# Decode attention on one core: K in whole 64 KB descriptors with two buffers, one V buffer, V through four column tiles, most of wo as rows

## The chip, the cores and the metric

The kernel runs on one core of a Trainium2 chip. The metric is the device time of one execution in microseconds. The kernel before takes 663.1 us. The experiments ran in four calls on different chips, each with the kernel before beside it (medians 663.20, 663.03, 663.14 and 663.18); the control of the changed kernel belongs to the first call alone. The profile of a run shows one of its executions, often the slowest.

## The reference

Two rows of one token each go through a pre-norm attention block with a cached K and V and then through a gated MLP:

```python
B, Sq, D = 2, 1, 512;  Hq = Hkv = 32;  Sk = 8192;  Dh = 128;  F = 1376       # bf16
q      = (layernorm(x) @ wq)                 # 32 heads of 128
scores = einsum("bhqd,bhkd->bhqk", q, k) * Dh ** -0.5
o      = einsum("bhqk,bhkd->bhqd", softmax(scores), v)
h      = x + o @ wo
n      = layernorm(h)
g      = n @ W_gate;  g = g * (g > 0)
out    = h + (g * (n @ W_up)) @ W_down
```

K and V together are 268 MB of the 281 MB that are read. Each element is used once.

## The kernel before

Four heads make a "quad": 8.4 MB of K and as much of V. 4 x 8192 keys lie over 128 partitions, T = 256 keys in each, so a quad of K or of V takes 64 KB of a partition; HT is half of T. There are N = 16 quads. A descriptor is one contiguous piece of a load, here what one partition gets; the trace shows each as a packet of that size. DVE multiplies K with the query and adds pairwise; ScalarE takes the exponential into `pm`; TensorE multiplies `pm` with V (of the two operands of a matmul, the stationary one is loaded first and the moving one streams past it). All loads are issued in program order by one queue (SP), and each waits there until its buffer is free (SPq in the views is that queue's sequencer).

```python
ring = ctx.enter_context(tc.tile_pool(name="ring", bufs=3))     # K, V, wq and the weights W by turns
...
def load_k(n):
    kts[n] = load(A_k_cache, n, (0, HT, T))                     # two DMAs, 32 KB a partition each
def load_v(n, cuts=(0, T)):
    vts[n] = load(A_v_cache, n, cuts)                           # one DMA, 64 KB a partition

def scores(n, k, lo, hi, between=None):                         # on half a quad
    ...
    nc.vector.tensor_tensor(out=kt[:, lo:hi, :], in0=kt[:, lo:hi, :], in1=<query>, op=ALU.mult)
    width = Dh
    while width > 8:
        half = width // 2
        nc.vector.tensor_tensor(<first half of width> += <second half>)
        width = half
    nc.vector.tensor_reduce(out=sc[:, 0:w], in_=<the last 8>, axis=AXIS.X, op=ALU.add)
    ...                                                         # exponentials into pm on ScalarE

def v_moving(n, o, lo, hi):                                     # V streams, pm is stationary
    for t in range(lo, hi, TG):                                 # TG = 4 keys of 4 heads: 16 columns
        ts = slice(t, t + TG)
        nc.tensor.matmul(out=o, lhsT=pm[:, ts, :].rearrange("p t h -> p (t h)"),
                         rhs=vt[:, ts, :].rearrange("p t d -> p (t d)"),
                         start=(t == 0), stop=(t == T - TG))
...
for n in range(N - 1):
    if n < N - 2:
        load_k(n + 1)
    scores(n, 0, 0, HT, between.get(n))
    scores(n, 1, HT, T)
    if n < N - 3:
        load_v(n + 1)
    ret = weighted_v(n)
    ...                                # at n == N - 3: V(N-2) and K(N-1) by halves, interleaved
...                                    # then wo, the last V in four pieces, W_gate, W_up, W_down
scores(N - 1, 0, 0, HT); scores(N - 1, 1, HT, CUTS[2], ...); scores(N - 1, 2, CUTS[2], T)
for i in range(LQ):
    for j in range(J):
        project(wo_sb[:, i, j, :], oc[:, i, j, :], ...)          # 4 x 28 matmuls of 2 columns
v_stationary(...)                                                # the last V, by pieces
...                                                              # second layernorm, MLP, store
```

The softmax here doesn't subtract the row's maximum and nothing guards it: scores larger than these inputs give would overflow.

## Time and profile before

| | before |
|---|---|
| time, median of 3 | 663.12 us (662.98 to 663.18) |
| span in the profile | 661.4 us |
| DMA busy, share of 16 engines | 99.0% |
| DVE busy | 603.0 us, 91% |
| TensorE busy | 295.7 us, 45% |

The first part of the profile page, as lines: busy time (share of the span) and instructions; then rows of the 40 slices, each digit the busy tenths of one slice (16.5 us); then the DMA packets and the queue that all loads use.

```profile
span 661.4 us, 4235 instructions
PE 295.7 (45%) x1704; PEld 132.7 (20%) x1704; DVE 603.0 (91%) x244; ACT 84.9 (13%) x329; POOL 4.7 (1%) x19
...
DVE  1698999999999999999999999999999999999991
...
DMA  9999999999999999999999999999999999999996
GB/s 381 444 444 411 450 406 442 428 449 444 398 443 426 450 414 453 418 426 442 415 462 409 430 442 421 452 414 447 420 428 444 425 460 400 436 424 436 412 410 256
DMA packets 10715, 281.32 MB, mean 425 GB/s; under 512 B 996, under 2 KB 1608, under 8 KB 4040
...
q1 hardware_dynamic: 10692, 281.06, 99.0%
```

Both rows are full of nines. Which of the two limits? Two views decide. The groups of instructions show in the last column how long an engine was idle just before, and for whom:

```profile
L251 PE MATMUL o<-kv,pm 128*16 128x512 bf16 x960 | 248.1, 424 | 322.4 <-DMA kv<-in_A_v_cache_dram 290.6
L202 DVE TENSOR_TENSOR kv<-kv,qrep 128x16384 bf16<-128x16384 bf16 (+2 forms) x33 | 278.1, 8427 | 29.3 <-DMA kv<-in_A_k_cache_dram 29.0
```

DVE and TensorE both wait for DMA. Does DMA wait for them? The queue's own table of waits (waiter, releaser: us in all, times, longest) seems to say yes:

```profile
SPq L183 <- DVE sc L217: 415.5, 14, 40.7
SPq L183 <- PE o L251: 124.0, 14, 10.4
```

But the sequencer that issues loads waits well before its engines run dry. The records of the single DMA packets, in the trace, settle it (this is a count over these records, not a view of the profile):

```
                              before
first packet starts           1.84 us
busy, mean of the 16 engines  654.8 us
first / last engine done      655.8 / 657.3 us
packets of 32 KB, median      1216 ns (x4608)
packets of 64 KB, median      2422 ns (x1792)
```

1.84 + 654.83 is 656.7, between the ends of the first and the last engine, so the engines had no idle time to speak of before their end. The end itself, in the timeline (start, length, engine, line, instruction; in brackets the idle time before it and what ended it):

```profile
650.82 1.71 PE L430 MATMUL gate_ps<-hd,W 128*128 128x2 bf16 x44 [0.25 <-DVE hd L416]
...
653.31 1.75 PE L430 MATMUL up_ps<-hd,W 128*128 128x2 bf16 x44 [0.35 <-DMA W<-in_B_W_up_dram]
...
656.93 0.99 PE L458 MATMUL y_ps<-act,W 128*128 128x2 bf16 x24 [0.80 <-DMA W<-in_B_W_down_dram]
...
659.39 0.30 SPq L476 DMA_DIRECT2D out_dram<-y_row  x1
```

The matmuls with W_gate (called the gate below) start at 650.82 us. Those with W_up and W_down wait for DMA, and some 4.5 us follow the last of these waits.

### The profile page before, as it was taken

To read this page: it belongs to the slowest core of one execution; us is meant where nothing else is said; L and a number is where in the kernel's file an instruction comes from. 1 tells how busy PE (TensorE), PEld (TensorE's weight loads), DVE (VectorE), ACT (ScalarE), POOL (GpSimd) and SP (SyncE) were. 2 spreads that over 40 slices of the span, in tenths; PEclk is the share of its full clock that TensorE was granted. 3 is DMA by queue.
4 is the path that set the end of the run, shared out by engine and by line. 5 is a ranking of instruction groups with operands and counts; after the bars stand their busy time and mean duration, and the time that the engine had idled before them with its cause. 6 is when DMAs were issued, how large, how long until landed. Compare 5 with 4: busy or idle time off the path is not lost.

```text
span 661.4 us, 4235 instructions
## 1 busy us (share of the span) xinstructions
PE 295.7 (45%) x1704; PEld 132.7 (20%) x1704; DVE 603.0 (91%) x244; ACT 84.9 (13%) x329; POOL 4.7 (1%) x19
## 2 busy tenths in 40 slices
PE   2108245090633608264370915537081552844346
PEld 1003112030211203122140301213030120311246
DVE  1698999999999999999999999999999999999991
ACT  2111101111101111110111110111111101111110
POOL 2000000000000000000000000000000000000000
PEclk9757669586776957777595867859586785956755
DMA  9999999999999999999999999999999999999996
GB/s 381 444 444 411 450 406 442 428 449 444 398 443 426 450 414 453 418 426 442 415 462 409 430 442 421 452 414 447 420 428 444 425 460 400 436 424 436 412 410 256
DMA packets 10715, 281.32 MB, mean 425 GB/s; under 512 B 996, under 2 KB 1608, under 8 KB 4040
## 3 DMA queue, kind: packets, MB, share of 16 engines
q1 hardware_dynamic: 10692, 281.06, 99.0%
q8 instruction: 13, 0.21, 0.1%
q14 instruction: 6, 0.05, 0.0%
q10 hardware_dynamic: 4, 0.00, 0.0%
HBM read 281.05 MB, written 0.00 MB: 425 GB/s over the span
## 4 chain that ended last, share of the span: by engine, by line
DVE 45%; DMA 41%; PE 8%; SPq 3%; ACT 2%; issue 1%; DVEq 0%
DMA kv<-in_A_k_cache_dram 34%; DVE kv L209 21%; DVE kv L202 21%; PE o L251 7%; DMA W<-in_A_wo_dram 3%; DVE sc L217 3%; SPq L370 3%; DMA W<-in_B_W_down_dram 2%; DMA wq_sb<-in_A_wq_dram 2%; ACT pm L234 2%; PE qps L164 1%; DVE ou L285 0%; SPq L376 0%; DVE rep L282 0%; PE y_ps L458 0%
## 5 line engine op out<-in xcount | busy, mean ns | idle before, releaser
L251 PE MATMUL o<-kv,pm 128*16 128x512 bf16 x960 | 248.1, 424 | 322.4 <-DMA kv<-in_A_v_cache_dram 290.6
L202 DVE TENSOR_TENSOR kv<-kv,qrep 128x16384 bf16<-128x16384 bf16 (+2 forms) x33 | 278.1, 8427 | 29.3 <-DMA kv<-in_A_k_cache_dram 29.0
L209 DVE TENSOR_TENSOR kv<-kv 128x8192 bf16<-128x8192 bf16 (+5 forms) x132 | 276.8, 2097 | 4.4
L251 PEld LDWEIGHTS <-pm 128*16 128x16 bf16 x960 | 91.9, 98 | 474.1 <-issue 295.8
L234 ACT ACTIVATE pm<-sc 32x128 bf16<-32x128 f32 (+1 forms) x128 | 61.6, 481 | 427.9 <-DVE sc L217 426.4
L217 DVE TENSOR_REDUCE sc<-kv 128x128 f32<-128x1024 bf16 (+2 forms) x33 | 39.2, 1188 | 3.3
L234 ACT ACTIVATION_READ_ACCUMULATOR pm<-sc 32x1 f32 x128 | 31.8, 248 | 0.0
L261 ACT ACTIVATE osb<-o,turn_of 16x128 f32<-16x128 f32 x60 | 16.6, 347 | 112.2 <-PE o L251 105.0
L275 PE MATMUL rep<-osb,head_of 16*128 16x128 f32 x112 | 17.2, 292 | 7.2 <-ACT osb L261 7.2
L275 PEld LDWEIGHTS rep<-osb,head_of 16*128 16x128 f32 x112 | 14.5, 183 | 14.2 <-ACT osb L261 13.1
L292 PE MATMUL o_b<-pm,kv 128*128 128x4 bf16 x256 | 7.4, 166 | 6.6 <-DMA kv<-in_A_v_cache_dram 6.6
L292 PEld LDWEIGHTS <-kv 128*128 128x128 bf16 x256 | 7.3, 105 | 6.9 <-DMA kv<-in_A_v_cache_dram 6.9
L386 PE MATMUL a_ps<-oc,W 128*128 128x2 bf16 x112 | 3.1, 165 | 11.7 <-DVE oc L313 11.7
L164 PE MATMUL qps<-wq_sb,xnb 128*32 128x512 bf16 x64 | 5.5, 517 | 4.5 <-DMA wq_sb<-in_A_wq_dram 4.5
L386 PEld LDWEIGHTS <-W 128*128 128x128 bf16 x128 | 3.7, 104 | 12.0 <-DMA W<-in_A_wo_dram 7.6
L164 PEld LDWEIGHTS <-xnb 128*32 128x32 bf16 x64 | 2.7, 119 | 6.9 <-issue 5.4
L430 PEld LDWEIGHTS <-W 128*128 128x128 bf16 (+1 forms) x88 | 3.4, 122 | 0.7 <-DMA W<-in_B_W_up_dram 0.4
L170 ACT ACTIVATE qrep<-qps 128x512 bf16<-128x512 f32 x4 | 2.4, 598 | 6.0 <-PE qps L164 6.0
L318 DVE RECIPROCAL zil<-zb 128x4 f32<-128x4 f32 x2 | 0.4, 178 | 2.9 <-PE zb L297 2.9
L137 PE MATMUL x_ps<-ident,x_row 2*128 2x2 bf16 x4 | 0.4, 173 | 5.8 <-DMA x_row<-in_A_x_dram 5.8
L297 PE MATMUL zb<-zl,mean_f 128*128 128x4 f32 x12 | 2.8, 354 | 0.0
L297 PEld LDWEIGHTS zb<-zl,mean_f 128*128 128x128 f32 x12 | 2.8, 329 | 0.0
(82 smaller groups left out, 40.5 us busy)
## 6 DMA issues: line engine op xcount, KB each, us to landing
kv<-in_A_k_cache_dram SPq DMA_DIRECT2D x32, 4096.0 KB, 32.3
kv<-in_A_v_cache_dram SPq DMA_DIRECT2D x3, 4096.0 KB, 21.3
wq_sb<-in_A_wq_dram SPq DMA_DIRECT2D x1, 4096.0 KB, 12.3
W<-in_A_wo_dram SPq DMA_DIRECT2D x1, 3584.0 KB, 21.2
kv<-in_A_v_cache_dram SPq DMA_DIRECT2D x1, 2560.0 KB, 26.0
W<-in_B_W_gate_dram SPq DMA_DIRECT2D x1, 1376.0 KB, 29.3
W<-in_B_W_up_dram SPq DMA_DIRECT2D x1, 1032.0 KB
kv<-in_A_v_cache_dram SPq DMA_DIRECT2D x1, 1024.0 KB, 27.2
```

Source lines behind the costliest of these rows:

```text
L164: nc.tensor.matmul(out=qps[h * Q:(h + 1) * Q], lhsT=xnb[:, c, b, :], rhs=wq_v[:, c, g:g + QP, h, :], start=(c == 0), stop=(c == KC - 1),)
L202: nc.vector.tensor_tensor(out=kt[:, lo:hi, :], in0=kt[:, lo:hi, :], in1=_view(qrep[:, b, i, :], 0, [[0, w], [1, Dh]]), op=ALU.mult)
L209: nc.vector.tensor_tensor(out=_view(kt, off, [[Dh, w], [1, half]]), in0=_view(kt, off, [[Dh, w], [1, half]]), in1=_view(kt, off + half, [[ ...
L217: nc.vector.tensor_reduce(out=sc[:, 0:w], in_=_view(kt, off, [[Dh, w], [1, 8]]), axis=AXIS.X, op=ALU.add)
L234: nc.scalar.activation(out=pm[ps, lo:hi, h], in_=sc[ps, 0:w], func=ACT.Exp, accum_out=(zm[ps, b, k, i:i + 1] if i < LQ else zl[ps, b, k, h ...
L251: nc.tensor.matmul(out=o, lhsT=pm[:, ts, :].rearrange("p t h -> p (t h)"), rhs=vt[:, ts, :].rearrange("p t d -> p (t d)"), start=(t == 0), ...
L261: nc.scalar.activation(out=osb[:, t, :], in_=o[:, t, :], func=ACT.Copy, scale=turn_of[:, t:t + 1])
L275: nc.tensor.matmul(out=reps[i // HQ][:, i % HQ, :], lhsT=head_of.rearrange("k h m -> k (h m)"), rhs=osb[:, t, :], start=(t == 0), stop=(t ...
L292: nc.tensor.matmul(out=o, lhsT=vt[:, t, :], rhs=pm[:, t, :], start=(t == 0), stop=(t == T - 1))
L297: nc.tensor.matmul(out=zb, lhsT=lhsT, rhs=z[:, k, :], start=(k == 0), stop=(k == 2))
L370: nc.sync.dma_start(out=wgu[:, g, c0:c1, :], in_=w.rearrange("(c p) n -> p c n", p=P)[:, c0:c1, :])
L386: nc.tensor.matmul(out=a_ps[:, c, :], lhsT=w[:, c * P:(c + 1) * P], rhs=o, start=(first and c == 0), stop=last, skip_group_check=True)
```

## The change

Its intent: K in whole loads, so in descriptors of 64 KB like V; two K buffers of their own, each refilled as soon as its scores are done, so that K runs a quad ahead of V; one buffer for V, made affordable by putting its matmuls through four column tiles of TensorE by turns (a tile is one of four groups of 32 output partitions, `g` in the code); DVE on whole quads (fewer instructions); and most of `wo` as 28 matmuls with 512 moving columns, also column-tiled, instead of 112 small ones. Core of the diff, cuts marked:

```diff
-    ring = ctx.enter_context(tc.tile_pool(name="ring", bufs=3))
+    kring = ctx.enter_context(tc.tile_pool(name="kring", bufs=2))
+    vring = ctx.enter_context(tc.tile_pool(name="vring", bufs=1))
 ...
-    def load_k(n):
-        kts[n] = load(A_k_cache, n, (0, HT, T))
+    def load_k(n):
+        kts[n] = kring.tile([P, T, Dh], bf16, tag="k", name="k")
+        load_part(kts[n], A_k_cache, n, 0, T)
 ...                                   scores(n, k, lo, hi, ...) becomes scores(n), on all of T
+    def clear(o):
+        nc.tensor.matmul(out=o, lhsT=<zeros>, rhs=<zeros>, start=True, stop=False, ...)
+
     def v_moving(n, o, lo, hi):
-        for t in range(lo, hi, TG):
+        for k, t in enumerate(range(lo, hi, TG)):
             ts = slice(t, t + TG)
-            nc.tensor.matmul(out=o, lhsT=pm[:, ts, :].rearrange("p t h -> p (t h)"),
+            g = k % (P // Q) * Q                       # column tile 0, 1, 2, 3, 0, ...
+            nc.tensor.matmul(out=o[g:g + G * TG], lhsT=pm[:, ts, :].rearrange("p t h -> p (t h)"),
 ...
     load_k(0)
+    load_k(1)
     load_v(0)
     for n in range(N - 1):
-        if n < N - 2:
-            load_k(n + 1)
-        scores(n, 0, 0, HT, between.get(n))
-        scores(n, 1, HT, T)
-        if n < N - 3:
-            load_v(n + 1)
+        scores(n)
+        if n + 2 < N:
+            load_k(n + 2)
         ret = weighted_v(n)
+        if n + 2 < N:
+            load_v(n + 1)
 ...
-    scores(N - 1, 0, 0, HT)
-    scores(N - 1, 1, HT, CUTS[2], most_of_last_row)
-    scores(N - 1, 2, CUTS[2], T)
-    for i in range(LQ):
-        for j in range(J):
-            project(wo_sb[:, i, j, :], oc[:, i, j, :], first=(i == 0 and j == 0))
+    scores(N - 1)
+    gather(HQ, LQ)
+    normalize(L, zb1)
+    ar_ps = ps_mm.tile([P, D], f32, tag="mm")
+    clear(ar_ps)
+    for k in range(LQ * J):                            # wo as rows, four column tiles
+        g = k % (P // Q) * Q
+        nc.tensor.matmul(out=ar_ps[g:g + B], lhsT=oc[:, k // J, k % J, :],
+                         rhs=wo_sb[:, k // J, k % J, :], start=False, ...)
+    ar = ...copy of ar_ps...
+    v_moving(N - 1, o15, 0, CUTS[1])
+    ...eight f32 matmuls bring ar back into a_ps...
+    v_moving(N - 1, o15, CUTS[1], CUTS[2])
 ...                                   the last 48 of 256 keys stay stationary, as before
```

More of the change, by code (lines that the diff above doesn't have):

```diff
@@ L59 @@
     misc = ctx.enter_context(tc.tile_pool(name="misc", bufs=1))
-    ring = ctx.enter_context(tc.tile_pool(name="ring", bufs=3))
-    spool = ctx.enter_context(tc.tile_pool(name="spool", bufs=2))
+    kring = ctx.enter_context(tc.tile_pool(name="kring", bufs=2))
+    vring = ctx.enter_context(tc.tile_pool(name="vring", bufs=1))
+    spool = ctx.enter_context(tc.tile_pool(name="spool", bufs=1))
     opool = ctx.enter_context(tc.tile_pool(name="opool", bufs=1))
@@ L68 @@
     mean_f = consts.tile([P, P], f32)
-    zm = consts.tile([P, B, 3, NQ - 1], f32)
-    zl = consts.tile([P, B, 3, G], f32)
+    zm = consts.tile([P, B, NQ - 1], f32)
+    zl = consts.tile([P, B, G], f32)
     eps_t = consts.tile([P, 1], f32)
@@ L80 @@
     masks.make_identity(nc, ident)
-    head_of = consts.tile([G * TG, G, Q], f32)
-    nc.gpsimd.memset(head_of, 0.0)
-    for t in range(TG):
-        nc.gpsimd.affine_select(out=head_of, in_=head_of, compare_op=ALU.not_equal, fill=1.0,
-                                base=-G * t, pattern=[[-1, G], [0, Q]], channel_multiplier=1)
-    turn_of = consts.tile([G * TG, TG], f32)
-    nc.gpsimd.memset(turn_of, 1.0)
+    head_of = consts.tile([P, G, Q], f32)
+    turn_of = consts.tile([P, TG], f32)
+    row_of = consts.tile([P, B], f32)
+    for t in (head_of, turn_of, row_of):
+        nc.gpsimd.memset(t, 0.0)
+    for g in range(P // Q):
+        for u in range(TG):
+            for t, base, pat in ((head_of, G * u, [[-1, G], [0, Q]]), (turn_of, u, [[-G, TG]])):
+                nc.gpsimd.affine_select(out=t, in_=t, compare_op=ALU.not_equal, fill=1.0,
+                                        base=-(Q * g + base), pattern=pat, channel_multiplier=1)
+        nc.gpsimd.affine_select(out=row_of, in_=row_of, compare_op=ALU.not_equal, fill=1.0,
+                                base=-Q * g, pattern=[[-1, B]], channel_multiplier=1)
+    zero = consts.tile([P, 1], bf16)
+    nc.gpsimd.memset(zero, 0.0)
     same = consts.tile([P, G, Q], f32)
     nc.gpsimd.memset(same, 1.0)
-    for t, pat, n in ((turn_of, [[G, TG]], G), (same, [[Q, G], [0, Q]], Q)):
-        neg = [[-s_, c_] for s_, c_ in pat]
-        nc.gpsimd.affine_select(out=t, in_=t, compare_op=ALU.is_ge, fill=0.0, base=0,
-                                pattern=neg, channel_multiplier=1)
-        nc.gpsimd.affine_select(out=t, in_=t, compare_op=ALU.is_ge, fill=0.0, base=n - 1,
-                                pattern=pat, channel_multiplier=-1)
-    mine = consts.tile([P, G], bf16)
-    nc.vector.tensor_copy(mine, same[:, :, 0])
+    nc.gpsimd.affine_select(out=same, in_=same, compare_op=ALU.is_ge, fill=0.0, base=0,
+                            pattern=[[-Q, G], [0, Q]], channel_multiplier=1)
+    nc.gpsimd.affine_select(out=same, in_=same, compare_op=ALU.is_ge, fill=0.0, base=Q - 1,
+                            pattern=[[Q, G], [0, Q]], channel_multiplier=-1)
     pick = consts.tile([P, Q], f32)
@@ L111 @@
     RING = T * Dh
-    wq_sb = ring.tile([P, RING], bf16, tag="s", name="wq_sb")[:, 0:KC * Hq * Dh].rearrange(
+    wq_sb = vring.tile([P, RING], bf16, tag="v", name="wq_sb")[:, 0:KC * Hq * Dh].rearrange(
         "p (c n) -> p c n", c=KC)
@@ L174 @@
     N = len(seq)
-    HT = T // 2
     LQ = NQ - 1
@@ L183, in load_part, with load_v, scores @@
         nc.sync.dma_start(out=t[:, lo:hi, :], in_=src[:, lo:hi, :])
-    def load(cache, n, cuts):
-        t = ring.tile([P, T, Dh], bf16, tag="s", name="kv")
-        for lo, hi in zip(cuts[:-1], cuts[1:]):
-            load_part(t, cache, n, lo, hi)
-        return t
-    def load_k(n):
-        kts[n] = load(A_k_cache, n, (0, HT, T))
-    def load_v(n, cuts=(0, T)):
-        vts[n] = load(A_v_cache, n, cuts)
-    def scores(n, k, lo, hi, between=None):
-        b, i = seq[n]
-        kt, w = kts[n], hi - lo
-        off = lo * Dh
-        nc.vector.tensor_tensor(out=kt[:, lo:hi, :], in0=kt[:, lo:hi, :],
-                                in1=_view(qrep[:, b, i, :], 0, [[0, w], [1, Dh]]), op=ALU.mult)
-        if between is not None:
-            between()
+    def load_k(n):
+        kts[n] = kring.tile([P, T, Dh], bf16, tag="k", name="k")
+        load_part(kts[n], A_k_cache, n, 0, T)
+    def load_v(n, cuts=(0, T)):
+        vts[n] = vring.tile([P, T, Dh], bf16, tag="v", name="v")
+        for lo, hi in zip(cuts[:-1], cuts[1:]):
+            load_part(vts[n], A_v_cache, n, lo, hi)
+    def scores(n):
+        b, i = seq[n]
+        kt = kts[n]
+        nc.vector.tensor_tensor(out=kt, in0=kt, in1=_view(qrep[:, b, i, :], 0, [[0, T], [1, Dh]]),
+                                op=ALU.mult)
         width = Dh
@@ L208, in scores @@
             half = width // 2
-            nc.vector.tensor_tensor(
-                out=_view(kt, off, [[Dh, w], [1, half]]),
-                in0=_view(kt, off, [[Dh, w], [1, half]]),
-                in1=_view(kt, off + half, [[Dh, w], [1, half]]),
-                op=ALU.add,
-            )
+            nc.vector.tensor_tensor(out=kt[:, :, 0:half], in0=kt[:, :, 0:half],
+                                    in1=kt[:, :, half:width], op=ALU.add)
             width = half
-        sc = spool.tile([P, HT], f32, name="sc")
-        nc.vector.tensor_reduce(out=sc[:, 0:w], in_=_view(kt, off, [[Dh, w], [1, 8]]),
-                                axis=AXIS.X, op=ALU.add)
+        sc = spool.tile([P, T], f32, name="sc")
+        nc.vector.tensor_reduce(out=sc, in_=kt[:, :, 0:8], axis=AXIS.X, op=ALU.add)
         pm = pms[n % NM]
-        if n == N - 1 and hi == T:
-            pd = misc.tile([P, w], bf16)
-            zd = misc.tile([P, 1], f32)
-            nc.scalar.activation(out=pd, in_=sc[:, 0:w], func=ACT.Exp, accum_out=zd,
-                                 scale=SCALE)
-            nc.vector.tensor_tensor(out=pm[:, lo:hi, :],
-                                    in0=pd.unsqueeze(2).to_broadcast([P, w, G]),
-                                    in1=_view(mine, 0, [[0, w], [1, G]]), op=ALU.mult)
-            nc.vector.tensor_tensor(out=zl[:, b, k, :], in0=same[:, :, 0],
-                                    in1=zd.to_broadcast([P, G]), op=ALU.mult)
-            return
         for h in range(G):
             ps = slice(h * Q, (h + 1) * Q)
-            nc.scalar.activation(out=pm[ps, lo:hi, h], in_=sc[ps, 0:w], func=ACT.Exp,
-                                 accum_out=(zm[ps, b, k, i:i + 1] if i < LQ
-                                            else zl[ps, b, k, h:h + 1]), scale=SCALE)
+            nc.scalar.activation(out=pm[ps, :, h], in_=sc[ps, :], func=ACT.Exp,
+                                 accum_out=(zm[ps, b, i:i + 1] if i < LQ else zl[ps, b, h:h + 1]),
+                                 scale=SCALE)
     oc = misc.tile([P, LQ, J, B], bf16)
@@ L244, with blocks_of @@
     reps = {}
+    def clear(o):
+        nc.tensor.matmul(out=o, lhsT=_view(zero, 0, [[0, P]]), rhs=_view(zero, 0, [[0, TG * Dh]]),
+                         start=True, stop=False, skip_group_check=True)
     def v_moving(n, o, lo, hi):
         vt, pm = vts[n], pms[n % NM]
-        for t in range(lo, hi, TG):
+        for k, t in enumerate(range(lo, hi, TG)):
             ts = slice(t, t + TG)
-            nc.tensor.matmul(out=o, lhsT=pm[:, ts, :].rearrange("p t h -> p (t h)"),
+            g = k % (P // Q) * Q
+            nc.tensor.matmul(out=o[g:g + G * TG], lhsT=pm[:, ts, :].rearrange("p t h -> p (t h)"),
                              rhs=vt[:, ts, :].rearrange("p t d -> p (t d)"),
-                             start=(t == 0), stop=(t == T - TG))
+                             start=False, stop=(t + P // Q * TG >= hi), skip_group_check=True)
+    def blocks_of(o):
+        osb = opool.tile([P, TG, Dh], f32, tag="row", name="osb")
+        for t in range(TG):
+            nc.scalar.activation(out=osb[:, t, :], in_=o[:, t * Dh:(t + 1) * Dh], func=ACT.Copy,
+                                 scale=turn_of[:, t:t + 1])
+        return osb
     def weighted_v(n):
         b, i = seq[n]
-        o = ps_o.tile([G * TG, TG, Dh], f32, tag="o", name="o")
+        o = ps_o.tile([P, TG * Dh], f32, tag="o", name="o")
+        clear(o)
         v_moving(n, o, 0, T)
-        osb = opool.tile([G * TG, TG, Dh], f32, tag="row", name="osb")
-        for t in range(TG):
-            nc.scalar.activation(out=osb[:, t, :], in_=o[:, t, :], func=ACT.Copy,
-                                 scale=turn_of[:, t:t + 1])
+        osb = blocks_of(o)
         if i == LQ:
@@ L292, in v_stationary @@
             nc.tensor.matmul(out=o, lhsT=vt[:, t, :], rhs=pm[:, t, :],
-                             start=(t == 0), stop=(t == T - 1))
+                             start=(t == CUTS[2]), stop=(t == T - 1), skip_group_check=True)
     def sum_z(zb, lhsT, z):
-        for k in range(3):
-            nc.tensor.matmul(out=zb, lhsT=lhsT, rhs=z[:, k, :], start=(k == 0), stop=(k == 2))
+        nc.tensor.matmul(out=zb, lhsT=lhsT, rhs=z, start=True, stop=True)
         return zb
@@ L334 @@
     load_k(0)
+    load_k(1)
     load_v(0)
     for n in range(N - 1):
-        if n < N - 2:
-            load_k(n + 1)
-        scores(n, 0, 0, HT, between.get(n))
-        scores(n, 1, HT, T)
-        if n < N - 3:
-            load_v(n + 1)
-        ret = weighted_v(n)
-        if n == N - 3:
-            vts[n + 1], kts[n + 2] = (ring.tile([P, T, Dh], bf16, tag="s", name="kv")
-                                      for _ in range(2))
-            for lo, hi in ((0, HT), (HT, T)):
-                load_part(vts[n + 1], A_v_cache, n + 1, lo, hi)
-                load_part(kts[n + 2], A_k_cache, n + 2, lo, hi)
+        if n in between:
+            between[n]()
+        scores(n)
+        if n + 2 < N:
+            load_k(n + 2)
+        ret = weighted_v(n)
+        if n + 2 < N:
+            load_v(n + 1)
         if n == NQ - 1:
@@ L353 @@
             zb0, zl0 = row_z(0, z0[:, 0:LQ]), last_z(0, z0[:, LQ:])
-    W = ring.tile([P, RING], bf16, tag="s", name="W")
+    W = kring.tile([P, RING], bf16, tag="k", name="W")
     wo_sb = W[:, 0:LQ * J * D].rearrange("p (i j n) -> p i j n", j=J, n=D)
@@ L366 @@
     nc.sync.dma_start(out=wol, in_=A_wo[LQ * G * Dh:, :].rearrange("(h d) n -> d h n", d=P))
-    CUTS = (0, HT, T * 13 // 16, T * 15 // 16, T)
+    CUTS = (0, T // 2, T * 13 // 16, T * 15 // 16, T)
     load_v(N - 1, CUTS)
@@ L382, with project @@
     a_ps = ps_acc.tile([P, KC, B], f32)
-    def project(w, o, first=False, last=False):
+    def project(w, o, last):
         for c in range(KC):
             nc.tensor.matmul(out=a_ps[:, c, :], lhsT=w[:, c * P:(c + 1) * P], rhs=o,
-                             start=(first and c == 0), stop=last, skip_group_check=True)
+                             start=False, stop=last, skip_group_check=True)
     L = B - 1
     zb1 = row_z(L, z_tile()[:, 0:LQ])
-    def most_of_last_row():
-        gather(HQ, LQ)
-        normalize(L, zb1)
-    scores(N - 1, 0, 0, HT)
-    scores(N - 1, 1, HT, CUTS[2], most_of_last_row)
-    scores(N - 1, 2, CUTS[2], T)
-    for i in range(LQ):
-        for j in range(J):
-            project(wo_sb[:, i, j, :], oc[:, i, j, :], first=(i == 0 and j == 0))
+    scores(N - 1)
[6 more added lines that the diff above has]
+        nc.tensor.matmul(out=ar_ps[g:g + B], lhsT=oc[:, k // J, k % J, :],
+                         rhs=wo_sb[:, k // J, k % J, :], start=False,
+                         stop=(k + P // Q >= LQ * J), skip_group_check=True)
+    ar = opool.tile([P, D], f32, tag="row")
+    nc.scalar.activation(out=ar, in_=ar_ps, func=ACT.Copy)
+    o15 = ps_o.tile([P, TG * Dh], f32, tag="o")
+    clear(o15)
+    v_moving(N - 1, o15, 0, CUTS[1])
+    for c in range(KC):
+        nc.tensor.matmul(out=a_ps[:, c, :], lhsT=ar[:, c * P:(c + 1) * P], rhs=row_of,
+                         start=(c == 0), stop=False, skip_group_check=True)
+    v_moving(N - 1, o15, CUTS[1], CUTS[2])
+    osb = blocks_of(o15)
     o_b = ps_o.tile([P, G], f32, tag="o", name="o_b")
-    v_stationary(N - 1, o_b, 0, CUTS[2])
     v_stationary(N - 1, o_b, CUTS[2], CUTS[3])
     zil = invert_last(L, last_z(L, z_tile()[:, 0:G]))
+    for t in range(TG):
+        nc.tensor.matmul(out=o_b, lhsT=osb[:, t, :], rhs=head_of[:, :, 0], start=False, stop=False,
+                         skip_group_check=True)
     v_stationary(N - 1, o_b, CUTS[3], T)
```

## The prediction

> **What bounds the kernel now.** The DMA queue. The page's slices show DMA at 9 tenths or more in 39 of 40, the queue table 99.0% of the span. By the trace's packet records the first packet starts at 1.84 us, each engine is busy 654.83 us, and the last W_down lands at about 656.9: 1.84 + 654.83 = 656.7, so there are no bubbles to speak of. Then 4.5 us of down projection, transpose and store follow (timeline). DVE is 91% busy, but its 29 us of waits on K (table of waits) are starvation: a quad costs DVE 37.5 us (chain of waits, 63.0 to 100.5), and DMA about 38.8 for its K and V.
>
> **What the change does.**
> - K in 64 KB descriptors. Packet medians: 1216 ns for 32 KB, 2422 for 64 KB (V has these already). Two of 32 KB cost 10 ns more than one of 64; 2176 pairs over 16 engines: 1.4 us, with fewer semaphore packets and hiccups some 0.2 more. The Trainium skill, "DMA: Bandwidth & Descriptors", Specifications, gives a fabric ceiling of 435 GB/s; the trace's 64 KB packets make 433, so little is left to win.
> - DVE in whole quads. Sizes 16384, 10240 and 6144 give a fixed cost of 0.15 us an instruction; six fewer, about 1 us a quad, 15 us in all. Off the critical path: DVE only waits longer for K.
> - V through column tiles. Now 32 matmuls 128x512 take 7.1 us warm, 9.7 cold. The Q projection, tiled so already, does 64 in 5.5 us. The Trainium skill, "TensorE: Matmul & The Clock Gate", Part 3, reports 2.38 times for three column tiles; the Q projection shows nearly four. A quad's V then takes 5.5 to 7 us after landing, hidden under the 19.4 us of K(n+2): this pays for having one V buffer.
> - K(n+2) needs scores(n) done before V(n) has landed. Tightest at the start, as DVE now starts when all of K(0) is in (32.5, was 22.9): scores(0) ends at 69, V(0) at 71.2, issue to first packet 1.0: margin 1 us. Next 3 us, then growing 2.3 us a quad. No bubble, or one under 1 us.
> - The end: the last V waits for V(14)'s matmuls (621) under 10.8 us of wo (to 625). The last scores end at 631.6 in one piece, so V no longer overlaps them; but tiled V, wo as rows (28 matmuls for 112) and 48 stationary matmuls give the gate's input at about 649, near the landing of W_gate (648.5). W_up (652) and W_down (655.3) still land last, and the same 4.5 us follow.
>
> **Prediction.** The DMA stream ends 1.5 us earlier: 661.6 us, range 660.7 to 663.4. Faster by over 2%: 0.01. Within 2%: 0.97. Slower by over 2%: 0.02.
>
> **What would show it.** About 2200 DMA packets fewer; DVE busy about 588 us, waiting longer on K; V matmuls near 100 ns apart; y_ps still waiting for W_down.
>
> **What would make it wrong.** DMA gaps between quads, if scores or V matmuls free buffers later than costed (V matmuls over 19 us a quad, over 9 for V(14)); or TensorE so late in the last quad that the gate starts after 650.5: each microsecond beyond is one of the time. A gain over 2% would need packets faster than 433 GB/s.

## The result, and the profile after

Ratios are the mean time of one kernel's runs over that of the other's in the same rounds, so they are not quite the ratio of the medians quoted.

| | before | after |
|---|---|---|
| first measurement, median | 663.05 us | 662.67 us (662.28 to 662.93); ratio 0.9994, interval 0.9976 to 1.0011 |
| again, with the experiments | 663.20 us | 662.51 us (662.34 to 662.64); ratio 0.9990, interval 0.9978 to 1.0002 |
| span in the profile | 661.4 us | 660.9 us |
| DMA busy, mean of 16 engines | 654.8 us | 653.9 us |
| DVE busy | 603.0 us | 588.0 us |
| TensorE busy | 295.7 us | 135.1 us |

The times are the same within 2%, as predicted. The medians are 0.4 and 0.7 us lower, where 1.5 was forecast; both intervals reach 1. The mean granted clock of TensorE is 0.71 in every run of the kernel before and 0.60 in every run of this one; it goes with the kernel. Page of the changed kernel, the lines that answer to those above:

```profile
span 660.9 us, 3558 instructions
PE 135.1 (20%) x1478; PEld 66.0 (10%) x1481; DVE 588.0 (89%) x139; ACT 74.4 (11%) x204; POOL 10.6 (2%) x51
...
DVE  1099999999999999999999998989899998999931
...
DMA  9999999999999999999999999999999999999996
GB/s 381 444 444 440 386 444 440 441 444 405 428 437 441 440 409 433 445 432 436 440 420 429 444 425 436 440 424 432 429 436 436 440 425 437 424 428 440 400 410 251
DMA packets 8264, 281.28 MB, mean 426 GB/s; under 512 B 724, under 2 KB 1336, under 8 KB 3768
...
q1 hardware_dynamic: 8244, 281.06, 98.9%
```

2451 packets fewer, and the mean rate goes from 425 to 426 GB/s. The groups:

```profile
L202 DVE TENSOR_TENSOR k<-k,qrep 128x32768 bf16<-128x32768 bf16 x16 | 275.5, 17220 | 37.1 <-DMA k<-in_A_k_cache_dram 37.1
...
L238 PE MATMUL o<-v,pm 128*16 128x512 bf16 x1012 | 90.4, 535 | 489.0 <-DMA v<-in_A_v_cache_dram 435.6
```

DVE's waits on K, before and then after (us in all, times, longest):

```profile
DVE kv L202 <- DMA kv<-in_A_k_cache_dram: 29.0, 12, 13.2
```

```profile
DVE k L202 <- DMA k<-in_A_k_cache_dram: 37.1, 9, 23.5
```

DVE saved 15 us. It starts ten us later (its first wait for K is 23.5 us instead of 13.2) and still ends its last scores at 632.3 us instead of 644.6. TensorE's V work fell from 248 us (without the last quad) to 90 (with most of it), and its wait for V rose from 291 to 436 us. Neither shows in the time. The queue's waits of the changed kernel:

```profile
SPq L187 <- DVE sc L211: 252.0, 14, 49.7
SPq L187 <- DMA v<-in_A_v_cache_dram: 238.8, 15, 21.4
SPq L187 <- PE o L238: 88.4, 15, 7.5
```

And its end:

```profile
650.82 1.72 PE L431 MATMUL gate_ps<-hd,W 128*128 128x2 bf16 x44 [0.25 <-DVE hd L417]
...
652.83 1.71 PE L431 MATMUL up_ps<-hd,W 128*128 128x2 bf16 x44
...
656.24 1.09 PE L459 MATMUL y_ps<-act,W 128*128 128x2 bf16 x24 [0.80 <-DMA W<-in_B_W_down_dram]
...
658.87 0.32 SPq L477 DMA_DIRECT2D out_dram<-y_row  x1
```

The last wait is still for W_down, 0.7 us earlier than before. From there to the end it took 4.7 us instead of 4.4, so the span fell by 0.4.

**Where the forecast gain went.** The packet records give the sum. "Base" is each packet at the lower median of its size in the two traces; "excess" is the rest:

```
                                before     after     after, measured again
base, us per engine             651.8      650.7     650.7
excess, 0 to 20 us              0.72       0.71      0.66
excess, 60 to 80 us             0.04       0.55      0.55
excess, all                     3.05       3.27      2.81
first / last engine done, us    655.8 / 657.3   655.0 / 656.5   654.7 / 656.6
```

At these medians larger packets and fewer semaphore packets are worth 1.1 us. That split is soft: the medians of the two traces are 3 ns apart for either size (1216 and 1213 ns, 2422 and 2419), and what the packets of the kernel before cost more by that stands in its excess. The total is firmer: without the excess of 60 to 80 us, the mean busy time fell by 1.4 us and, measured again, by 1.9, about the 1.6 that the prediction added up. Of this 0.5 us is given back at one place: near 70 us, the first packets of K(2) take 2745 to 3156 ns instead of 2420, in 15 of the 16 engines. The timeline shows K(2) issued there, the moment scores(0) end:

```profile
66.88 2.29 DVE L211 TENSOR_REDUCE sc<-k 128x256 f32<-128x2048 bf16 x1
69.08 17.22 DVE L202 TENSOR_TENSOR k<-k,qrep 128x32768 bf16<-128x32768 bf16 x1
69.19 0.33 SPq L187 DMA_DIRECT2D k<-in_A_k_cache_dram  x1
...
72.43 6.57 PE L238 MATMUL o<-v,pm 128*16 128x512 bf16 x64 [53.40 <-ACT pm L215]
...
79.06 0.33 SPq L187 DMA_DIRECT2D v<-in_A_v_cache_dram  x1
```

V(0), the load ahead of it, ends at 70.4 us (median of the engines): a margin of 1.2 us. The queue never looks idle, since packets start at once, but these take longer. The rest is lost at the end: the mean busy time fell by 0.9 and 1.3 us in the two profiles, the end of the last engine by 0.8 and 0.7, the span by 0.4 and 0.5. The experiments below turn the margin into a rule for this kernel.

### The profile page after: what moved, and what is told of

It is laid out like the page before. It is cut to its first block, busy times and chain, and to the rows that moved or that the text cites. A ratio compares the mean times of both kernels' runs of the same rounds, so it can differ in the third digit from the quotient of the medians. Undisturbed runs are those within 1.5% of the kernel's fastest.

```text
span 660.9 us, 3558 instructions
## 1 busy us (share of the span) xinstructions
PE 135.1 (20%) x1478; PEld 66.0 (10%) x1481; DVE 588.0 (89%) x139; ACT 74.4 (11%) x204; POOL 10.6 (2%) x51
## 4 chain that ended last, share of the span: by engine, by line
DVE 60%; DMA 36%; SPq 3%; issue 0%; PE 0%; DVEq 0%
DMA k<-in_A_k_cache_dram 29%; DVE k L202 29%; DVE k L207 28%; DMA W<-in_A_wo_dram 5%; DVE sc L211 4%; SPq L364 3%; DMA W<-in_B_W_down_dram 2%; DVE ou L278 0%; DVE rep L275 0%; PE yt_ps L470 0%; PE y_ps L459 0%; DVE y_row L476 0%; SPq L119 0%; SPq L352 0%; DVEq L211 0%
## 5 line engine op out<-in xcount | busy, mean ns | idle before, releaser
L202 DVE TENSOR_TENSOR k<-k,qrep 128x32768 bf16<-128x32768 bf16 x16 | 275.5, 17220 | 37.1 <-DMA k<-in_A_k_cache_dram 37.1
L207 DVE TENSOR_TENSOR k<-k 128x16384 bf16<-128x16384 bf16 (+1 forms) x64 | 266.1, 4158 | 2.2
L238 PE MATMUL o<-v,pm 128*16 128x512 bf16 x1012 | 90.4, 535 | 489.0 <-DMA v<-in_A_v_cache_dram 435.6
L238 PEld LDWEIGHTS <-pm 128*16 128x16 bf16 x1012 | 33.1, 117 | 543.5 <-ACT pm L215 294.0
L215 ACT ACTIVATE pm<-sc 32x256 bf16<-32x256 f32 x64 | 49.2, 768 | 261.1 <-DVE sc L211 260.4
L246 ACT ACTIVATE osb<-o,turn_of 128x128 f32<-128x128 f32 x64 | 18.3, 368 | 293.9 <-PE o L238 287.2
L211 DVE TENSOR_REDUCE sc<-k 128x256 f32<-128x2048 bf16 x16 | 36.6, 2286 | 1.6
L268 PE MATMUL rep<-osb,head_of 128*128 128x128 f32 x112 | 17.8, 301 | 7.5 <-ACT osb L246 7.5
L268 PEld LDWEIGHTS rep<-osb,head_of 128*128 128x128 f32 x112 | 15.0, 188 | 14.5 <-ACT osb L246 14.5
L215 ACT ACTIVATION_READ_ACCUMULATOR pm<-sc 32x1 f32 x64 | 15.9, 249 | 0.0
```

The lines of the kernel that those rows point to most:

```text
L202: nc.vector.tensor_tensor(out=kt, in0=kt, in1=_view(qrep[:, b, i, :], 0, [[0, T], [1, Dh]]), op=ALU.mult)
L207: nc.vector.tensor_tensor(out=kt[:, :, 0:half], in0=kt[:, :, 0:half], in1=kt[:, :, half:width], op=ALU.add)
L211: nc.vector.tensor_reduce(out=sc, in_=kt[:, :, 0:8], axis=AXIS.X, op=ALU.add)
L215: nc.scalar.activation(out=pm[ps, :, h], in_=sc[ps, :], func=ACT.Exp, accum_out=(zm[ps, b, i:i + 1] if i < LQ else zl[ps, b, h:h + 1]), sc ...
L238: nc.tensor.matmul(out=o[g:g + G * TG], lhsT=pm[:, ts, :].rearrange("p t h -> p (t h)"), rhs=vt[:, ts, :].rearrange("p t d -> p (t d)"), s ...
L246: nc.scalar.activation(out=osb[:, t, :], in_=o[:, t * Dh:(t + 1) * Dh], func=ACT.Copy, scale=turn_of[:, t:t + 1])
```

## The experiments

Theory A: the time is the end of the DMA stream on its slowest engine plus some 4.5 us. The change moves only the stream: it is 1.4 to 1.9 us shorter, but for a thin margin at the start that costs 0.5. Theory B, the rival: the kernel is limited by DVE and TensorE as well (DVE busy 89%; after the change the chain that ended last is put down to DVE for 60%), and their gains and losses cancel. That line of the two pages, before and then after, is what makes B plausible:

```profile
DVE 45%; DMA 41%; PE 8%; SPq 3%; ACT 2%; issue 1%; DVEq 0%
```

```profile
DVE 60%; DMA 36%; SPq 3%; issue 0%; PE 0%; DVEq 0%
```

### The changed kernel again

No edit: the control of the next three runs.

> The changed kernel again, as control for the three other kernels of this call. Both theories: 662.7 us, within 0.3, and 0.4 below the kernel before. Theory A (DMA stream alone): the time is the moment of the last W_down landing plus 4.6 us. Theory B (co-limited): DVE's saving of 15 us and the later, longer last quad cancel each other, and the small DMA gain is beside the point.

662.51 us, before 663.20 beside it. As expected for a control; 0.7 below the kernel before this time.

### first_split: the first K in halves

```diff
-        load_part(kts[n], A_k_cache, n, 0, T)
+        for lo, hi in (((0, T // 2), (T // 2, T)) if n == 0 else ((0, T),)):
+            load_part(kts[n], A_k_cache, n, lo, hi)
 ... and the same two pieces, for n == 0 only, around multiply, adds and reduce in scores(n)
```

> The changed kernel with K(0) loaded in two halves and its products, sums and reduce in two halves, so that scores(0) ends near 60 us instead of 69 and K(2) is issued ten us before the queue runs dry. Theory A: the 15 or so packets near 70 us that took about 3000 ns go back to 2420; the stream shortens by 0.55 us less one 32 KB load (0.05): 0.5 us faster than the control. Rival C (64 KB packets are slower when all loads have them): those packets stay slow, no gain. Theory B: DVE starts ten us earlier, so its end is earlier by up to ten, and the time falls by more than 1 us.

662.22 us (661.92 to 662.36), ratio to before 0.9985, interval 0.9973 to 0.9997. K(2) is issued nine us earlier:

```profile
60.56 0.33 SPq L187 DMA_DIRECT2D k<-in_A_k_cache_dram  x1
```

The excess between 60 and 80 us falls from 0.55 to 0.05 us, and the engines' mean busy time and last end fall by 0.2 and 0.6 us against the control. The time falls by 0.3 us, a little less than the 0.5 expected. That is A: the slow packets came from the late issue, not from packet size (rival C), and DVE's ten us earlier start are worth nothing by themselves (B expected more than 1 us).

### k_halves: K in 32 KB descriptors again

```diff
-        load_part(kts[n], A_k_cache, n, 0, T)
+        load_part(kts[n], A_k_cache, n, 0, T // 2)
+        load_part(kts[n], A_k_cache, n, T // 2, T)
```

> The changed kernel with each K loaded by two DMAs of 32 KB a partition, all else as it is. Theory A: 2048 packets of 64 KB become 4096 of 32 KB, 7 to 13 ns more a pair over 16 engines: 0.9 to 1.7 us, 0.15 of semaphore packets: 1.0 to 1.9 us slower than the control, so slower than the kernel before. Theory B: no difference, as DVE and TensorE see the same data at the same time.

664.70 us (663.51 to 665.00), ratio to before 1.0019: 2.2 us slower than the control, just above the 1.0 to 1.9 expected, and slower than the kernel before. The records: base time 1.04 us more; the late issue of K(2) costs 0.5 us more than in the control, now as idle engines; and the 16 engines end further apart (655.9 to 659.1 us, where the control had 654.7 to 656.6). The last one counts. So the term of the packets alone, 1.04 us, is at the low end of what A says; the rest came with the later K(2) and with engines that end further apart, as one profile shows (of the slowest of the five runs; their times spread over 1.5 us). With 32 KB descriptors the rest of the change would have been a loss of 1.5 us against the kernel before.

### loop_one_tile: quads 0 to 14 without column tiles

```diff
-            g = k % (P // Q) * Q
+            g = k % (P // Q) * Q if n == N - 1 else 0
```

> The changed kernel with all V matmuls of quads 0 to 14 in one column tile (the last quad still takes four). Theory A: 64 matmuls then take 15 to 18 us, more than twice as long, yet under 19.4, so that no gap opens in the loop; but the last V waits for V(14)'s matmuls to about 632 while wo is through at about 625: a gap of 7 to 8 us in the DMA, and the time is 7 to 8 us longer (669.5 to 671). Theory B, if TensorE shares the limit all along: 10 us more in every quad, over 50 us in all.

680.05 us (676.79 to 683.43), ratio 1.0249: 17.5 us slower, where A expected 7 to 8 and B over 50. The matmuls took what was expected (timeline of TensorE):

```profile
466.53 16.88 PE L238 MATMUL o<-v,pm 128*16 128x512 bf16 x64 [22.08 <-DMA v<-in_A_v_cache_dram]
...
505.50 16.18 PE L238 MATMUL o<-v,pm 128*16 128x512 bf16 x64 [20.09 <-DMA v<-in_A_v_cache_dram]
```

and the gap before the last V is there (the engines lack 9.8 us between 620 and 645). What was wrong is "no gap opens in the loop". The queue's timeline around one quad:

```profile
483.44 0.33 SPq L187 DMA_DIRECT2D v<-in_A_v_cache_dram  x1
483.86 0.38 SPq L187 DMA_DIRECT2D k<-in_A_k_cache_dram  x1
```

The K ahead of this V had ended at 483.0 us, by the median engine. Counting each load of the trace so (margin: end of the load ahead less start of the issue; load: from that end to its own; a load with time enough takes 19.33 us):

```
issue     margin    load     lost
128.45     0.40     20.76    1.43
207.51     0.61     20.50    1.17
285.79     1.34     19.93    0.60
402.40     1.78     19.48    0.15
442.49     0.49     20.64    1.31
483.44    -0.45     21.63    2.30
521.71     2.25     19.33    0.00
559.89     2.74     19.34    0.01
the changed kernel, K(2):
69.19      1.21     19.92    0.59
```

A load loses about 1.9 us less its margin, and with more than some 2 us nothing beyond the scatter. (The medians over the engines leave a scatter of some 0.4 us: margins of 2.1 and 3.1 us lost 0.5 and 0.3, and in the changed kernel some loads with margins of 9 to 20 us lost 0.3 to 0.4.) V(1) to V(14) lost 9.0 us in all. The spread of the engines takes part of each margin: the matmuls that end just before the issue at 483.44 us began at 466.5, when the last engine had ended its V at 466.1; the median engine had at 463.6. The prediction called a margin of 1 us "no bubble, or one under 1 us"; it had taken 1.0 us for the issue off already, so its 1 us is 2 us here, which this table prices at next to nothing. In the loop, then, column tiles are no gain in time by themselves but the condition for one V buffer.

### v_half_less: 4.2 MB less to load

```diff
         vts[n] = vring.tile([P, T, Dh], bf16, tag="v", name="v")
+        if n == NQ - 1:
+            cuts = (0, T // 2)
 ...
+            vs = slice(t % (T // 2), t % (T // 2) + TG) if n == NQ - 1 else ts
-                             rhs=vt[:, ts, :].rearrange("p t d -> p (t d)"),
+                             rhs=vt[:, vs, :].rearrange("p t d -> p (t d)"),
```

> The changed kernel with only the first half of V(7) loaded and used twice (a wrong result on purpose): 4.2 MB of 281 less, all instructions of DVE, ScalarE and TensorE as they are. Theory A (the DMA stream sets the time): 128 packets of 64 KB become 32 KB ones, 9.7 us less in the stream, and the time falls by all of it: 652.9 us, 652.4 to 653.4, since DVE has 13.6 us of waits on K left after the start. Theory B (DVE is a co-limit): less than half of it.

653.12 us (652.86 to 653.37), ratio 0.9850, against 652.9 expected. (The comparison with the reference still passes, presumably because with nearly even weights over 8192 keys the attention's share of the output is too small to show in its tolerance. It is wrong all the same.) Of the 9.7 us, 9.4 arrive against the control and 9.6 against the first measurement, with every other engine's work unchanged; its DVE waits 29.2 us on K instead of 37.1. This is the clearest sign for A.

### dve_more and dve_much_more: extra DVE work in quads 2 to 14

```diff
         nc.vector.tensor_reduce(out=sc, in_=kt[:, :, 0:8], axis=AXIS.X, op=ALU.add)
+        if 2 <= n < N - 1:                                      # 64 in dve_more, 256 in dve_much_more
+            nc.vector.tensor_reduce(out=sc[:, 0:64], in_=kt[:, 0:64, 0:8], axis=AXIS.X, op=ALU.add)
```

> The changed kernel with a quarter of the last reduce done twice in quads 2 to 14: 13 x 0.69 us, 9 us more of DVE. Theory A: DVE's waits on K fall from 13.6 us (after the first) to about 5 and the time stays within 0.4 us. Theory B: some 9 us slower.

> The same with the whole last reduce done twice in quads 2 to 14: 13 x 2.29 = 29.8 us more. Theory A: 13.6 us of it hide in the waits, the last scores end 16 us later (648 instead of 632), of which TensorE's waits for the last V take up some 3: 12 us slower than the changed kernel, 672 to 677. Theory B: all of it, 30 us slower.

dve_more: 662.76 us (662.40 to 663.07), ratio 0.9996. It is 0.3 us below the kernel before, where the changed kernel was 0.4 and 0.7 below: of 9 us of extra work at most some 0.4 show. dve_much_more: 672.06 us (671.77 to 672.60), ratio 1.0138: 9.5 us for 29.7 us of work, at the low edge of the range expected. Their waits on K, first of dve_more, then of dve_much_more:

```profile
DVE k L202 <- DMA k<-in_A_k_cache_dram: 29.4, 6, 23.2
```

```profile
DVE k L202 <- DMA k<-in_A_k_cache_dram: 23.0, 1, 23.0
```

The changed kernel waits 37.1 us, 23.5 of them for the first K. So 13.6 us are slack; in the second run only the wait for the first K is left, DVE has become the limit and its last scores end at 647.9 us instead of 632.3. Of these 15.6 us the span shows 9.1: the gate starts only 10.4 us later (661.20), chiefly as TensorE no longer waits for the last V, and from there 1.3 us of waits for W_down are gone. A is right for the kernel as it is, and the slack is finite: less than 1 us a quad.

### last_one_tile: the last quad without column tiles

```diff
-            g = k % (P // Q) * Q
+            g = k % (P // Q) * Q if n < N - 1 else 0
```

> The changed kernel with the V matmuls of the last quad alone in one column tile: 32 matmuls of 2.3 us become 7 to 9 us, 20 of 1.3 us become 4.4. The DMA is untouched and its stream ends when it did. Theory A allows this: the last quad's TensorE has only about half a microsecond to spare before the gate, so the gate starts 5 to 7 us later and the time is 5 to 7 us longer (667.5 to 669.5), with the last DMA landing unmoved at 656 to 657.

665.32 us (664.22 to 666.22), ratio 1.0033: 2.8 us slower than the control, less than the 5 to 7 expected. The four runs fall into two pairs, near 664.3 and 666.2, for a reason not looked into; the profile is of the slower pair. Timeline:

```profile
637.67 7.97 PE L238 MATMUL o<-v,pm 128*16 128x512 bf16 x32
...
646.56 4.48 PE L238 MATMUL o<-v,pm 128*16 128x512 bf16 x20
...
655.58 1.72 PE L431 MATMUL gate_ps<-hd,W 128*128 128x2 bf16 x44 [0.25 <-DVE hd L417]
```

The matmuls took what was expected, 8.9 us more than the 2.29 and 1.26 us of the changed kernel, and the end of the last engine stayed (656.9 us, 656.5 in the changed kernel). But the gate started only 4.8 us later, as TensorE's waits for V's pieces were used up first, and from the gate to the end it took 1.3 us less, as the waits for W_down vanished: 3.5 us in the span. The gate thus had 1.3 us to spare, and the V matmuls of the last quad more, where the expectation gave them half a microsecond. In the last quad column tiles do save time.

### wo_columns: wo as 112 small matmuls again

```diff
-    for k in range(LQ * J):                   # 28 matmuls into ar_ps, a copy, eight f32 matmuls
-        ...
+    for k in range(LQ * J):
+        project(wo_sb[:, k // J, k % J, :], oc[:, k // J, k % J, :], last=False, first=(k == 0))
```

> The changed kernel with its rows form of wo undone: 112 matmuls of two columns into a_ps, as before, in place of 28 of 512 columns, a copy and eight f32 matmuls. From the traces: before's 112 took 3.1 us, the 28 took 3.2 and the eight 1.05. Theory A: TensorE is free one to two microseconds earlier, and waits that much longer for V's part up to 13/16 of the last quad (it waited 2.0 us for it); no change, within 0.3 us of the changed kernel. If the rows form is worth something, this is slower.

662.29 us (662.13 to 662.75), ratio 0.9989, interval 0.9975 to 1.0002: no difference from the changed kernel that these runs resolve. The rows form of `wo` is worth nothing here; its 28 matmuls took 3.16 us where before's 112 had taken 3.13.

### before_whole_k: one part of the change alone

```diff
-        kts[n] = load(A_k_cache, n, (0, HT, T))
+        kts[n] = load(A_k_cache, n, (0, T))
```

(on the kernel before)

> The kernel before with one part of the change alone: each K in one load of 64 KB a partition; its ring of three and its half-quad scores are as before. Theory A says that a load costs time when it is issued less than about 1.9 us before the load ahead of it ends (as the other runs show). Here V(n+1) waits for scores(n), which now start only when all of K(n) is in: 37.5 us of DVE in a DMA period of 38.8, a margin of about 1 us, in each quad. Some 0.5 us is lost in each of 14 quads against 1.4 won by the packets: 4 to 8 us slower than before. If packet size were all that mattered it would be 1.4 us faster.

689.10 us (688.81 to 690.23), ratio 1.0395: 26 us slower. The sign and the cause are as expected, the size is not. The timeline of V(2)'s issue and of DVE's next start:

```profile
110.33 0.33 SPq L183 DMA_DIRECT2D kv<-in_A_v_cache_dram  x1
...
114.48 8.69 DVE L202 TENSOR_TENSOR kv<-kv,qrep 128x16384 bf16<-128x16384 bf16 x1 [4.17 <-DMA kv<-in_A_k_cache_dram]
```

The load of K(2) ended on its first engine at 110.3 us and on its last at 114.1. DVE can start only then. The expectation had one number for the end of a load; the spread of the engines, 0.5 to 3.8 us in this run, comes off the margin. Measured margins of the V loads are -1.2 to 1.5 us, and 13 of them lose 0.9 to 3.2 us each, 22.8 us in all; two half loads near the end lose 4.0 more, and packets win 1.0 back, which makes the 26. This is why the change cannot be had by its descriptors alone: in the ring of three, V(n+1) needs scores(n), and scores(n) need all of K(n). Two K buffers and a quad of lead go with margins of 9 us and more from K(5) to the last load of the loop in the changed kernel. No run takes the two K buffers, or DVE's whole quads, alone.

### fewer_small and fewer_small_2: attempts to beat both

fewer_small adds to first_split: W_gate and W_up as contiguous rows of 11 KB a partition (with the hidden vector laid out to match), the smallest piece of W_down first, and the last sum of exponentials earlier:

```diff
-    for g, w, c0, c1 in ((0, B_W_gate, 0, KC), (1, B_W_up, 0, KC - 1), (1, B_W_up, KC - 1, KC)):
-        nc.sync.dma_start(out=wgu[:, g, c0:c1, :],
-                          in_=w.rearrange("(c p) n -> p c n", p=P)[:, c0:c1, :])
+    for g, w in ((0, B_W_gate), (1, B_W_up)):
+        nc.sync.dma_start(out=wgu[:, g].rearrange("p c n -> p (c n)"),
+                          in_=w.rearrange("(p c) n -> p (c n)", p=P))
 ... lhsT columns taken as "(m c)", residual in the same order, wd_l loaded and used first
```

> An attempt to beat both: the changed kernel with the first K in halves (as in first_split), W_gate and W_up in contiguous rows of 11 KB a partition (256 packets for 1024), the small last piece of W_down loaded before its other pieces, and the last quad's sum of exponentials moved ahead of its wait. Theory A: 0.5 us from the start, 0.6 from the packets, 0.2 at the very end: 661.2 us, 660.7 to 661.8. It would be nearer 662 if TensorE's chain (gate at 650.8) becomes the later of the two.

662.47 us (662.22 to 662.58), ratio 0.9989: no gain. The mean busy time of the engines did fall, to 652.7 us, but the last engine ended at 656.0 as in first_split (the spread grew from 1.8 to 2.5 us), TensorE waited 0.8 us for W_up as one load, and the two last copies, now with a strided destination, took 0.7 us instead of 0.4. The second attempt mended these two:

```diff
+    for g, w, c0, c1 in ((0, B_W_gate, 0, KC), (1, B_W_up, 0, KC - 1), (1, B_W_up, KC - 1, KC)):
+        ...in_=w.rearrange("(p c) n -> p (c n)", p=P)[:, c0 * F:c1 * F]
 ... the result transposed as eight matmuls of 64 columns, copied in two contiguous pieces
```

> The kernel of fewer_small with its two own costs mended: W_up in two loads again, so that TensorE need not wait for all of it (it waited 0.8 us), and the result written to SBUF in contiguous pieces (its two copies took 0.7 us where they had taken 0.4). Theory A: the stream is shorter by some 1 us, and now the end follows it: 661.7 us, 661.2 to 662.2. If it stays at 662.3 or above, TensorE's chain of the last quad has become what the end waits for, and the gain of the packets is lost behind it.

662.41 us (662.21 to 662.89), ratio 0.9989: a miss. In its profiled run, the slowest of the five (662.89), the mean busy time was 653.2 us, the last engine ended at 656.4, and TensorE still waited for W_down (0.56 us), so its chain was not what the end waited for, as the expectation offered; the slowest engine was, 0.4 us later than in first_split, and the eight transposes then took 1.0 us where four had taken 0.6. That is read from one profile of each. What makes one engine later than the others was not tested and stays open. The lowest time of all kernels is first_split's, 1.0 us below the kernel before (0.15%); wo_columns and fewer_small_2 are 0.8 to 0.9 below the kernel before, a difference from first_split that these runs hardly resolve.

## Why the prediction was right

It was right in its kind, and large in its size: 1.5 us forecast, 0.4 and 0.7 measured. That the time lies in its range says little, since the range, 660.7 to 663.4, holds the kernel before as well. What tests it is the mechanism, and there two terms of the sum were off: the margin of K(2), taken as free, cost 0.5 us, and the end of the stream, taken as one moment, did not follow the mean of the engines.

- "The DMA queue" bounds the kernel: shown. 4.2 MB less are 9.4 to 9.6 us less, 9 us of DVE more cost at most some 0.4.
- "Some 15 us in all. Off the critical path": 15.0 us saved (603.0 to 588.0), none seen in the time. The prediction did not say how much slack that leaves; dve_much_more does: 13.6 us, under 1 us a quad.
- "A quad's V then takes 5.5 to 7 us": 4.9 to 6.6 in the trace. What was to show the mechanism did: 2451 packets fewer (2200 forecast), V matmuls 77 to 103 ns apart on average (near 100), and y_ps still waits for W_down.
- "1.4 us, with fewer semaphore packets and hiccups some 0.2 more" (hiccups are packets slower than their median): borne out in sum. Without the slow packets near 70 us the mean busy time fell by 1.4 and 1.9 us, and by 1.6 in first_split. How much of it is the size of the packets is less sure: 7 ns a pair at the medians of the changed kernel, 10 at those of the kernel before.
- "Margin 1 us ... No bubble, or one under 1 us": it cost 0.5 us, and the headline of 1.5 us took it as nothing. The forecast had V(0) end at 71.2 us and took 1.0 off for the issue. Its last engine did end at 71.0, but the median engine at 70.4, so in the forecast's own count the margin was 0.2 us for most engines (1.2 in the count used above). And the first packets of a load issued so late take about 0.6 to 0.8 us longer, so that 1.9 us are needed from issue to the end of the load ahead. First_split brought it back.
- One end for all 16 engines was assumed. The last engine ended 1.5 us after the first in the kernel before and 1.5 and 1.9 us after it in the two profiles of the changed kernel, so that of 0.9 and 1.3 us of mean busy time 0.8 and 0.7 came through to the last engine, and 0.4 and 0.5 to the span. In first_split 1.6 became 1.3 and 1.1. The spread matters more in k_halves, before_whole_k and fewer_small.
- "So late in the last quad that the gate starts after 650.5: each microsecond beyond is one of the time": the gate started at 650.8, not at 649, and it cost nothing: W_down was still waited for. In the kernel before it had started at 650.8 too, so the limit of 650.5 was set too early. last_one_tile shows 1.3 us of slack behind the gate.
- The two citations: the 435 GB/s of the Trainium skill hold as a ceiling (433 in 64 KB packets; a slice of the page counts each packet where it starts, so single slices read up to 462). For column tiles, one tile took 15.3 to 16.9 us for 64 matmuls and four took 4.9 to 6.6, so 2.3 to 3.4 times over a group. Start for start it is the full four times: in the slow beginning of a group four matmuls start in each 0.427 us and later in each 0.216 us, where one tile starts one. A group gains less than that because most of a four-tile group falls into its slow beginning (some 36 of the 64 in the group at 460.4 us), of a one-tile group only a few (14 in the one at 466.5 us).

## What to carry to other kernels

When the DMA engines are busy throughout, price a change by bytes, by packet time and by the moment at which the last engine ends, and treat savings on other engines only as slack. Check for each load how long before the end of its predecessor it is issued: in this kernel less than about 2 us costs time though no engine looks idle, and a buffer scheme must leave that margin plus the spread of the engines. A chain of waits that names another engine for 60% does not show that this engine limits; adding work to it tells.

## What the Trainium skill lacked or had wrong

- "DMA: Bandwidth & Descriptors", Specifications and Latency and other measured facts: it gives some 0.6 us to the first byte for loads issued by the sync queue. That agrees here if counted from the end of the issuing instruction (1.21 us, first packet at 1.84); from its start it is 1.0 us. What the page lacks is a number for a queue that stays full: a load behind a busy queue had to be issued about 1.9 us before its predecessor's end to lose nothing (margin 1.2 us lost 0.6, 0.4 lost 1.4, -0.45 lost 2.3).
- The same page, Rules for kernel authors, asks for 1 MiB and more per DMA. Beyond that, bytes per descriptor still count, if little: 2 x 1216 ns for 32 KB against 2422 in the kernel before, 2 x 1214 against 2421 in k_halves; undoing it for K cost 2.2 us of 662.5, spread of the engines included.
- The same page, "Why a DMA increments its semaphore by 16 and not by 1", says that the engines finish independently. It gives no size: the ends of one load lie 0.5 to 3.8 us apart in before_whole_k, and where no load is late they carry over from load to load (1.9 to 2.1 us from V(1) to V(13) in the kernel before).
- The same page, "Where 436 GB/s comes from", says that HBM, at about 358 GB/s, binds for loads into SBUF. This core alone ran at 425 to 426 GB/s over the whole span, so the sentence does not hold for a core that runs alone; the page's own table of measurements has 425 GB/s for 16 MB on a single core.
- "TensorE: Matmul & The Clock Gate", Part 3, has a rate for three column tiles (2.38 times) but none for four taken by turns in a real loop: 64 matmuls of 512 columns in 4.9 to 6.6 us against 15.3 to 16.9 us in one tile.
